# One load instead of two for the first weight block, a reordered row of small bias loads, and a later parameter transpose in a fused SSM + MLP kernel

## The chip, the cores and the metric

One core of a Trainium2 chip. The metric is the device time of one execution in microseconds (us), smaller is better. The sets of rounds ran on different chips (three are on record, and the median of the kernel before differs between them, 213.67 to 214.03 us), so times are compared within one set, and across sets only by their ratios.

"Traced" means one execution recorded by the hardware profiler. Times in a trace count from the start of its span. In all traced executions here the device time is the span plus 1.3 to 1.4 us.

## The reference

```python
# x: [1, 2048, 640] bf16; g is a gate for each row; a a complex diagonal SSM; b an MLP
g = sigmoid((x * gate_w).sum(-1, keepdims=True))
a = 2 * Re(h_seq @ C^T) + x * Dskip,  h_t = Lam_bar * h_{t-1} + B_bar @ x_t
b = gelu(x @ w1 + b1) @ w2 + b2       # w1: [640, 1728], w2: [1728, 640]
out = g * a + (1 - g) * b
```

`Lam_bar` and `B_bar` are worked out on chip from three vectors of 640 values (`Lambda_re`, `Lambda_im`, `log_dt`). These and `b1` are loaded as rows of one tile, `rows`, and turned into columns by one TensorE transpose, called the parameter transpose below.

## The kernel before

A small list scheduler orders the instructions on each engine by `prio` and by its own estimates, and puts waits where tiles depend on each other. (A semaphore is a counter: each DMA engine that moves a part of a load adds 1 to it when its part is done, in these traces 16 for a W1 block, 13 for b1's rows and 2 for the bias row, and the load has landed when the last one has.) What matters is the start: which loads are issued on which queue and in which order, and where in TensorE's order the parameter transpose stands.

```python
load("xna", "sp", ..., xn[0][:, :, 0:256], x2[0:512, 0:256]..., prio 0)
for h in range(2):                      # W1 block 0 (128 rows x 1024) in two loads, 1 KB pieces
    fs = slice(h * FW // 2, (h + 1) * FW // 2)
    load(f"w1_0{h}", "sp", ..., W1sb[:, 0, fs], B_w1[0:128, fs], [("w1", 0, h)], 0.1 + h, ...)
w1load(1, "sp", 1.3)                    # blocks 1 to 4: one load each, 2 KB pieces
w1load(2, "sp", 2)
xtrans(0, range(KN, KD), 3, 1.8)        # DMA transpose of x into xT, k = 2..4
w1load(3, "sp", 4)
w1load(4, "sp", 5)
# ... cut ...
# ACT queue: Lambda_re, Lambda_im, log_dt (5 rows each), b1 (13 rows), bias row b1b (1 row, 2 pieces)
load(nm, "act", "l_" + nm, rows[r0:...], src, [nm], prio=-100 + i, dur=0.4)
load("b1b", "act", "l_b1b", rows[RT:RT + 1, :]..., ["b1b"], prio=-96, dur=0.4)
# ... cut ...
op("cols", "pe", 0.3, list(ROWS) + ["b1b", "ident"], [("bank", 7)], f_cols, prio=9.5)  # parameter transpose
# ... cut: the first product x @ w1, 40 matmuls, k outermost, jf (8 PSUM banks) inside
op(f"m1_0_{jf}_{k}", "pe", d_mm(512), XK0[k] + [("w1", k) if k else ("w1", 0, jf // (NW // 2))], ...)
```

The first two k blocks of xT come from TensorE transposes of `xn`; k = 2 to 4 come from the DMA transpose. The parameter transpose uses PSUM bank 7, so it must stand ahead of the 15th matmul of the first product (called m1 here), which is the first to write that bank. At `prio` 9.5 it stands after 9 m1 matmuls. (One matmul is out of the k order: the one of bank 7 at k = 0 is put off to just before that of k = 1. So the first 7 matmuls need block 0, the 8th to 14th block 1, and the 17th is the first that needs block 2 and the DMA transpose of x.)

## Time and profile before

213.85 us median (213.85 to 213.9, 3 runs). The traced execution took 214.2 us, span 212.9 us.

| engine | busy us | share of the span |
|---|---|---|
| TensorE (PE) | 208.4 | 98% |
| VectorE (DVE) | 188.9 | 89% |
| ScalarE (ACT) | 111.3 | 52% |

From the profile page of the kernel before: the busy line and the first line of the chain that ended last.

```profile
PE 208.4 (98%) x1254; PEld 119.8 (56%) x1264; DVE 188.9 (89%) x262; ACT 111.3 (52%) x201; POOL 2.5 (1%) x10
PE 95%; DMA 2%; issue 1%; ACTq 1%; POOL 0%; DVE 0%; POOLq 0%
```

The list of waits of the kernel before, for TensorE (engine and line, what it waited for: us in total, times, longest):

```profile
PE ps L401 <- PEq L962: 0.8, 1, 0.8
PE ps L621 <- DMA W1sb<-in_B_w_dram: 0.4, 2, 0.2
PE ps L432 <- DMA rows<-in_B_b_dram: 0.3, 1, 0.3
PE ps L684 <- issue: 0.2, 1, 0.2
PE ps L621 <- DVE xT L419: 0.2, 1, 0.2
```

TensorE is the limit, and nearly all of its waits fall in the first 8 us. The timeline of the kernel before, TensorE from 3 us (start us, us, engine, line, operation, tiles, count, idle before and its releaser):

```profile
3.74 0.65 PE L413 MATMUL ps<-ident,xn 128*128 128x128 bf16 x8
4.64 1.04 PE L621 MATMUL ps<-xT,W1sb 128*128 128x512 bf16 x4 [0.25 <-DVE xT L419]
5.85 0.82 PE L621 MATMUL ps<-xT,W1sb 128*128 128x512 bf16 x3 [0.17 <-DMA W1sb<-in_B_w_dram]
6.92 0.61 PE L621 MATMUL ps<-xT,W1sb 128*128 128x512 bf16 x2 [0.25 <-DMA W1sb<-in_B_w_dram]
7.82 0.22 PE L432 MATMUL ps<-ident,rows 128*128 128x128 bf16 x1 [0.29 <-DMA rows<-in_B_b_dram]
7.87 6.85 PE L621 MATMUL ps<-xT,W1sb 128*128 128x512 bf16 x30
```

Four m1 matmuls, a gap, three, a gap, two, a gap, the parameter transpose, and from there on an unbroken stretch (L621 is m1, L432 the transpose). The timeline of the two issuing queues of the kernel before, for the first loads; consecutive loads of one tile are merged (x4 are W1's two halves, block 1 and block 2):

```profile
1.25 1.97 SPq L326 DMA_DIRECT2D W1sb<-in_B_w_dram  x4
3.27 1.54 SPq L333 DMA_TRANSPOSE xT<-in_A_x_dram  x1
0.97 0.57 ACTq L326 DMA_DIRECT2D rows<-in_A_Lambda_re_dram  x1
2.22 1.06 ACTq L326 DMA_DIRECT2D rows<-in_B_b_dram  x2
```

The last two of the ACT queue are b1's 13 rows (issued at 2.22) and the bias row (2.60).

### The profile page before, as it was taken

What the parts mean: (1) busy time and instruction counts of PE and PEld (TensorE: products, weight loads), DVE (VectorE), ACT (ScalarE), POOL (GpSimd) and SP (SyncE); (2) the same over time, 40 slices, a digit from 0 to 9 for tenths busy, and PEclk for the clock granted to TensorE, in tenths of its full rate; (3) what the DMA queues carried; (4) which work ended last, traced back from release to release, by engine and by line L of the source; (5) the groups of instructions that cost most, each with busy time, mean ns of one, the idle gap of its engine ahead of it and who ended that gap; (6) DMA issues with size and microseconds to landing.
All of it is one profiled execution on the core that took longest, in us unless ns stands there. A gap on an engine that the chain in (4) does not pass through costs nothing.

```text
span 212.9 us, 3113 instructions
## 1 busy us (share of the span) xinstructions
PE 208.4 (98%) x1254; PEld 119.8 (56%) x1264; DVE 188.9 (89%) x262; ACT 111.3 (52%) x201; POOL 2.5 (1%) x10
## 2 busy tenths in 40 slices
PE   8899999999999999999999999999999999999996
PEld 3344444444467776444466777544446777767773
DVE  2399999999999999999999959999999998999343
ACT  2389556678915324556963233555793444723330
POOL 1000000000000010000000001000000000000000
DMA  5999999998100004100000004000000000000011
GB/s 134 298 284 200 170 208 318 265 222 183 22 0 3 31 31 126 62 0 0 0 3 0 0 34 155 31 31 3 0 0 2 3 31 31 31 3 31 31 34 62
DMA packets 31434, 16.35 MB, mean 77 GB/s; under 512 B 22972, under 2 KB 30652, under 8 KB 31420
## 3 DMA queue, kind: packets, MB, share of 16 engines
q1 hardware_dynamic: 31072, 14.83, 29.2%
q0 software_dynamic: 288, 1.31, 1.9%
q8 instruction: 10, 0.16, 0.3%
q14 instruction: 4, 0.03, 0.0%
q10 hardware_dynamic: 60, 0.01, 0.0%
HBM read 7.63 MB, written 2.62 MB: 48 GB/s over the span
## 4 chain that ended last, share of the span: by engine, by line
PE 95%; DMA 2%; issue 1%; ACTq 1%; POOL 0%; DVE 0%; POOLq 0%
PE ps L771 27%; PE ps L641 22%; PE ps L819 20%; PE ps L684 20%; PE ps L621 3%; DMA rows<-in_B_b_dram 2%; PE ps L785 1%; PE ps L662 1%; ACTq L326 1%; DVE osb L852 0%; POOL io_i L382 0%; PE ps L432 0%; POOL rows L372 0%; POOL st_i L384 0%; POOL st_i L383 0%
## 5 line engine op out<-in xcount | busy, mean ns | idle before, releaser
L771 PE MATMUL ps<-W2sb,Gl 128*128 128x320 bf16 x416 | 59.2, 299 | 0.0
L771 PEld LDWEIGHTS ps<-W2sb,Gl 128*128 128x128 bf16 x416 | 40.3, 98 | 17.1 <-issue 1.1
L641 PE MATMUL ps<-xT,W1sb 128*128 128x512 bf16 x215 | 47.5, 379 | 0.3
L819 PE MATMUL ps<-CT,H 128*128 128x320 bf16 (+2 forms) x320 | 45.4, 299 | 0.0
L724 DVE TENSOR_TENSOR_SCAN W<-atab,V 128x1280 bf16<-128x1280 f32 x16 | 44.3, 2811 | 0.3
L684 PE MATMUL ps<-xT,BT 128*128 128x512 bf16 x196 | 43.1, 379 | 0.3 <-issue 0.2
L819 PEld LDWEIGHTS ps<-CT,H 128*128 128x128 bf16 x320 | 31.3, 98 | 12.2
L799 ACT ACTIVATE E<-ps,g1col 128x320 bf16<-128x320 f32 x32 | 16.3, 526 | 39.7 <-PE ps L771 26.0
L641 PEld LDWEIGHTS ps<-xT,W1sb 128*128 128x128 bf16 x220 | 21.5, 98 | 26.0
L648 ACT ACTIVATE Gl<-ps,cols 128x512 bf16<-128x512 f32 x44 | 29.6, 688 | 10.0 <-PE ps L641 10.0
L684 PEld LDWEIGHTS ps<-xT,BT 128*128 128x128 bf16 x200 | 19.5, 98 | 23.5 <-ACT Gt L670 0.4
L693 ACT ACTIVATE U<-ps 128x512 bf16<-128x512 f32 x40 | 23.8, 597 | 15.0 <-PE ps L684 14.9
L830 ACT ACTIVATE E<-ps,gcol 128x320 bf16<-128x320 f32 x30 | 15.8, 527 | 22.6 <-PE ps L819 22.6
L482 DVE TENSOR_TENSOR osb<-xg,E 128x640 bf16<-128x640 bf16 x15 | 7.3, 487 | 9.2 <-ACT E L830 8.2
L758 ACT ACTIVATE ps<-b2b 128x320 f32<-128x320 bf16 x32 | 14.1, 442 | 1.1
L838 DVE SCALAR_TENSOR_TENSOR xg<-xn,gcol,dsk 128x640 bf16<-128x640 bf16 x16 | 13.9, 883 | 0.4
L598 DVE SCALAR_TENSOR_TENSOR scr<-xn,gwb 128x640 bf16<-128x640 bf16 x16 | 13.2, 823 | 0.4
L482 DVE TENSOR_TENSOR V<-V,W 128x1280 bf16<-128x1280 bf16 x16 | 12.5, 822 | 0.3
L482 DVE TENSOR_TENSOR H<-H,V 128x1280 bf16<-128x1280 bf16 x16 | 12.5, 822 | 0.3
L482 DVE TENSOR_TENSOR V<-mr,U 128x2560 bf16<-128x2560 bf16 x8 | 11.9, 1489 | 0.2
L482 DVE TENSOR_TENSOR H<-c,W 128x2560 bf16<-128x2560 bf16 x8 | 11.9, 1489 | 0.1
L482 DVE TENSOR_TENSOR V<-s,W 128x2560 bf16<-128x2560 bf16 x8 | 11.9, 1485 | 0.0
(79 smaller groups left out, 98.5 us busy)
## 6 DMA issues: line engine op xcount, KB each, us to landing
out_dram<-osb SPq DMA_DIRECT2D x15, 160.0 KB, 1.8
W2sb<-in_B_w_dram SPq DMA_DIRECT2D x1, 2080.0 KB, 9.4
xn<-in_A_x_dram POOLq DMA_DIRECT2D x2, 640.0 KB, 4.7
W1sb<-in_B_w_dram SPq DMA_DIRECT2D x4, 256.0 KB, 4.8
xn<-in_A_x_dram SPq DMA_DIRECT2D x1, 640.0 KB, 8.0
W1sb<-in_B_w_dram SPq DMA_DIRECT2D x1, 480.0 KB, 5.7
W1sb<-in_B_w_dram SPq DMA_DIRECT2D x1, 400.0 KB, 5.8
xn<-in_A_x_dram SPq DMA_DIRECT2D x1, 384.0 KB, 6.2
```

What stands on the lines that cost most here:

```text
L482: return inc("dve", nc.vector.tensor_tensor(out=o, in0=a, in1=b, op=o_))
L641: t = nc.tensor.matmul(PS[bank][:, :], W1sb[:, k, jf * 128:(jf + 1) * 128], xT[q][:, k, :], start=(k == 0), stop=(k == KD - 1))
L648: return inc("act", nc.scalar.activation(Gl[q % 2][:, jf, :], PS[bank][:, :], ACT.Gelu_apprx_tanh, bias=b1col[:, jf:jf + 1]))
L684: t = nc.tensor.matmul(PS[bank][:, :], BT[:, ci, kd, k * 128:(k + 1) * 128], xT[q][:, kd, :], start=(kd == 0), stop=(kd == KD - 1))
L693: return inc("act", nc.scalar.activation(dst, src, ACT.Copy, scale=1.0 if ci == 0 else -1.0))
L724: t = inc("dve", nc.vector.tensor_tensor_scan(out=g[:, ci, :], data0=a, data1=v[:, ci, :], initial=0.0, op0=ALU.mult, op1=ALU.add))
L758: return inc("act", nc.scalar.activation(PS[bank][:, 0:HALF], b2b[:, cols], ACT.Copy))
L771: t = nc.tensor.matmul(PS[bank][:, 0:HALF], Gl[q % 2][:, jf, t4 * 128:(t4 + 1) * 128], W2sb[:, jf, cols], start=False, stop=False, skip_gr ...
L799: return inc("act", nc.scalar.activation(E1[c % NE][:, cols], PS[bank][:, 0:HALF], ACT.Copy, scale=g1col[:, c:c + 1]))
L819: t = nc.tensor.matmul(PS[bank][:, 0:n], H[b % NHB][:, ci, k, s * 128:(s + 1) * 128], CT[:, ci, k, cols], start=(i == 0), stop=(i == 2 * K ...
L830: return inc("act", nc.scalar.activation(E2[c % NE][:, cols], PS[bank][:, 0:HALF], ACT.Copy, scale=gcol[:, c:c + 1]))
L838: return inc("dve", nc.vector.scalar_tensor_tensor(out=xg[c % 2][:, :], in0=xn[q % 2][:, c % 4, :], scalar=gcol[:, c:c + 1], in1=dsk[:, :] ...
```

## The change

The intent: read W1's first block in longer pieces and with one issue fewer, get the single-row bias load out of the way early, and give the parameters two matmuls more time before TensorE has to wait for them.

```diff
-        for h in range(2):
-            fs = slice(h * FW // 2, (h + 1) * FW // 2)
-            load(f"w1_0{h}", "sp", f"l_w10{h}", W1sb[:, 0, fs], B_w1[0:128, fs], [("w1", 0, h)], 0.1 + h, dur=0.45, lat=2.0)
+        w1load(0, "sp", 1)
 ...
-             B_b1[nmain:F]...broadcast_to([1, 2, FL]), ["b1b"], prio=-96, dur=0.4)
+             B_b1[nmain:F]...broadcast_to([1, 2, FL]), ["b1b"], prio=-101, dur=0.4)
 ...
-        op("cols", "pe", 0.3, list(ROWS) + ["b1b", "ident"], [("bank", 7)], f_cols, prio=9.5)
+        op("cols", "pe", 0.3, list(ROWS) + ["b1b", "ident"], [("bank", 7)], f_cols, prio=11.5)
 ...   # m1 waits for the whole of block 0
-                op(f"m1_0_{jf}_{k}", ..., XK0[k] + [("w1", k) if k else ("w1", 0, jf // (NW // 2))], ...)
+                op(f"m1_0_{jf}_{k}", ..., XK0[k] + [("w1", k)], ...)
```

At the start, the order of instructions differs in just these points: one W1 load fewer on SP, the bias row first instead of last on ACT, and the parameter transpose after 11 instead of 9 m1 matmuls.

More of the change, by code (lines that the diff above doesn't have):

```diff
@@ L378, in bass_gated_mix__ssm_conv_s5__dense_activation_gelu__prompt_kernel @@
         load("b1b", "act", "l_b1b", rows[RT:RT + 1, :].rearrange("o (a p) -> o a p", a=2),
-             B_b1[nmain:F].rearrange("(o p) -> o p", o=1).unsqueeze(1).broadcast_to([1, 2, FL]), ["b1b"], prio=-96, dur=0.4)
+             B_b1[nmain:F].rearrange("(o p) -> o p", o=1).unsqueeze(1).broadcast_to([1, 2, FL]), ["b1b"], prio=-101, dur=0.4)
         def f_iota():
@@ L622, in f_mm @@
                                                       start=(k == 0), stop=(k == KD - 1)))
-                op(f"m1_0_{jf}_{k}", "pe", d_mm(512), XK0[k] + [("w1", k) if k else ("w1", 0, jf // (NW // 2))], [("bank", jf)] ,
+                op(f"m1_0_{jf}_{k}", "pe", d_mm(512), XK0[k] + [("w1", k)], [("bank", jf)] ,
                    f_mm, prio=pe_prio())
@@ L643, in f_mm @@
                     return inc("pe", t)
-                op(f"m1_{q}_{jf}", "pe", KD * d_mm(512), XT[q] + ([("w1", 0, 0), ("w1", 0, 1)] + [("w1", k) for k in range(1, KD)] if jf < NW else [("w1", "r", int(jf * 128 >= FM))]), [("bank", bank)], f_mm, prio=pe_prio())
+                op(f"m1_{q}_{jf}", "pe", KD * d_mm(512), XT[q] + ([("w1", k) for k in range(KD)] if jf < NW else [("w1", "r", int(jf * 128 >= FM))]), [("bank", bank)], f_mm, prio=pe_prio())
                 def f_ge(jf=jf, bank=bank):
```

## The prediction

> **What bounds the kernel.** TensorE. The page's busy table gives PE 208.4 of 212.9 us (98%), and the chain that ended last is 95% PE. The list of waits shows only five PE waits, all in the first 8 us: 0.8 us before the warm-up, then 0.25 (VectorE's copy of xT), 0.2 + 0.2 (W1 loads) and 0.3 (the load into `rows`). From the parameter transpose at 7.82 us on, PE runs practically without a gap up to the tail at 210.8 us. So only the start can pay, and at most about 1 us of it (idle from 4.39 to 7.87 us: 0.25 + 0.17 + 0.25 + 0.29), under 0.5% of the time.
>
> **The start, before** (timeline and landing records): xn part lands at 3.70; W1 block 0, first half 4.03, second half 5.81; block 1 6.87; block 2 7.56; xT's DMA transpose 9.05. PE: 4 matmuls at 4.64, 3 at 5.85, 2 at 6.92, parameter transpose at 7.82 (the single-row bias landed at 7.68, 4.4 us after its issue ended), then dense at 0.22 us each; the 12th m1 matmul starts near 8.31.
>
> The packet records show the bias row's two packets already running at 6.07 and 6.41 us, but its semaphore reaching its count only at 7.63/7.68, while the DMA transpose's first packets on all engines stand still from about 6.4 to 7.35. The Trainium skill, "DMA: Bandwidth & Descriptors", section on queues, rings and completion order, says that the completing increment lands only after every earlier write of that engine, across its queues; the trace agrees.
>
> **What the change does.** It removes one SP issue (0.42 us, spacing 0.54), so W1 blocks 1 and 2 and the DMA transpose are issued about 0.5 us earlier. 256 pieces of 1 KB (46 ns each) become 128 of 2 KB (84 ns): 0.74 to 0.67 us per engine, little. But the first m1 matmul now needs the whole block instead of its first half: I expect it to land at 4.6 to 5.6 us instead of 4.03, so PE starts m1 later (near 5.1), then runs 7 matmuls without the 5.68 gap. The bias row becomes early (near 3 us); b1's 13 rows become last, issued near 2.6 us, and land behind block 2 and the DMA transpose's stall, near 7.2 us. The transpose then stands after 11 matmuls.
>
> Estimate: 7 matmuls from 5.1 end at 6.7; block 1 near 6.5; four more end near 7.6; transpose 0.1 us more; 12th m1 matmul near 7.85 instead of 8.31. Gain near 0.4 us. The following matmuls need xT's DMA transpose (17th matmul, near 9.0 against landing 8.6 to 9.05), which caps it. Afterwards PE is the limit, so the gain should arrive at the end unchanged; VectorE's parameter chain starts at the same time or slightly earlier than 8.07 and has slack (1.0 us of ACT idle before the first gelu).
>
> **Prediction: 213.5 us, 80% range 213.0 to 214.1.** Faster by over 2%: 0.003; within 2%: 0.99; slower by over 2%: 0.007.
>
> **Right or wrong:** the first m1 matmul starts after 4.64 (W1 as releaser); no gap between matmuls 4 and 5; the transpose's release is W1 or the b1 load near 7.2 to 7.6; dense PE from there; the first gelu about 0.4 us earlier than 13.25; everything later shifted by that constant.
>
> **What would make it wrong:** the one-load block lands near the old second half's 5.81, cancelling the gain; b1's rows, spread on 13 engines, catch a straggler and land after 8 us, making it slower; the xT transpose becomes a new wait at the 17th matmul; or the stall is shorter and the gain nearer 0.8 us.

## The result, and the profile after

213.93 us median (213.69 to 214.44, 4 runs), against 213.85 us (213.47 to 213.9, 4 runs) before: ratio 1.0011, 95% interval 0.9989 to 1.0032. Here and below a ratio is made from the runs of both kernels in the same rounds; it is not quite the ratio of the medians quoted.

The time lies in the predicted range, but the gain of 0.4 us, the point of the argument, is not there. The trace alone would have said otherwise: its span is 212.6 us against 212.9. But the traced execution of the kernel before took 214.2 us, 0.35 us more than its median; that of the changed kernel, 213.91 us, is a usual one. The page of the changed kernel (busy line and chain):

```profile
PE 208.7 (98%) x1254; PEld 120.3 (57%) x1264; DVE 189.2 (89%) x262; ACT 111.3 (52%) x201; POOL 2.5 (1%) x10
PE 95%; DMA 2%; ACTq 1%; issue 1%; POOL 0%; DVE 0%; POOLq 0%
```

The list of waits of the changed kernel, TensorE, and its timeline from 3 us:

```profile
PE ps L399 <- PEq L960: 0.8, 1, 0.8
PE ps L430 <- DMA rows<-in_B_b_dram: 0.3, 1, 0.3
PE ps L682 <- issue: 0.2, 1, 0.2
```

```profile
3.69 1.03 PE L411 MATMUL ps<-ident,xn 128*128 128x128 bf16 x8
4.68 2.94 PE L619 MATMUL ps<-xT,W1sb 128*128 128x512 bf16 x11
7.97 0.22 PE L430 MATMUL ps<-ident,rows 128*128 128x128 bf16 x1 [0.35 <-DMA rows<-in_B_b_dram]
8.03 6.42 PE L619 MATMUL ps<-xT,W1sb 128*128 128x512 bf16 x28
```

The two W1 waits are gone from the list, and the wait for a row load is still there. And the eight small transposes at L411 take 1.03 us where before they took 0.65: TensorE ran at half speed there. The queues of the changed kernel:

```profile
1.26 1.62 SPq L326 DMA_DIRECT2D W1sb<-in_B_w_dram  x3
2.92 2.01 SPq L333 DMA_TRANSPOSE xT<-in_A_x_dram  x1
0.97 1.19 ACTq L326 DMA_DIRECT2D rows<-in_B_b_dram  x1
3.22 0.33 ACTq L326 DMA_DIRECT2D rows<-in_B_b_dram  x1
```

The bias row's issue takes 1.19 us at the head of the queue (Lambda_re in that place took 0.57), so b1's 13 rows, now last, are issued at 3.22 us, 0.62 us later than the last load before, and behind the DMA transpose instead of ahead of it. When the loads land, by the semaphore records of the two traces (time of the last DMA engine's increment):

| us | before | changed |
|---|---|---|
| W1 block 0 | 4.03 and 5.81 (halves) | 4.30 |
| W1 block 1 | 6.87 | 6.54 |
| W1 block 2 | 7.56 | 7.28 |
| last row load | 7.68 (bias row) | 7.73 (b1's 13 rows) |
| xT, DMA transpose | 9.05 | 8.79 |
| 12th m1 matmul starts | 8.30 | 8.03 |
| first B projection matmul starts | 19.95 | 19.68 |

The B projection is what TensorE does after the first product. From its first matmul to the end of the span it took 192.91 to 192.93 us in every one of the 14 traces. So the whole effect of any of these kernels is one number: when the B projection starts. The device time is that number plus 194.2 to 194.3 us.

### The profile page after: what moved, and what is told of

It reads as the page before. It is cut to its first block, busy times and chain, and to the rows that moved or that the text cites. A ratio compares the mean times of both kernels' runs of the same rounds, so it can differ in the third digit from the quotient of the medians.

```text
span 212.6 us, 3112 instructions
## 1 busy us (share of the span) xinstructions
PE 208.7 (98%) x1254; PEld 120.3 (57%) x1264; DVE 189.2 (89%) x262; ACT 111.3 (52%) x201; POOL 2.5 (1%) x10
## 4 chain that ended last, share of the span: by engine, by line
PE 95%; DMA 2%; ACTq 1%; issue 1%; POOL 0%; DVE 0%; POOLq 0%
PE ps L769 27%; PE ps L639 22%; PE ps L817 20%; PE ps L682 20%; PE ps L619 3%; DMA rows<-in_B_b_dram 2%; PE ps L783 1%; PE ps L660 1%; ACTq L326 1%; DVE osb L850 0%; POOL io_i L380 0%; PE ps L430 0%; POOL rows L370 0%; POOL st_i L382 0%; POOL st_i L381 0%
```

## The experiments

Three theories were on the table. **A**: the gain is real and comes from two matmuls moved ahead of a wait whose end hardly moves; the wait is for whatever row load stands last in the ACT queue. **B**: the difference of the two traces is scatter. **C** (later): the reordering and the one-load block work against each other. "Before" stands for the kernel before, on the same chip in the same rounds.

### The two kernels again

No edit. `before_again` expected:

> The kernel before, unchanged, to see how far two executions of one kernel differ. Theory A (the change shifts TensorE's dense stretch by a fixed 0.27 us, because two matmuls move ahead of a wait of nearly unchanged end): the second m1 group again starts at 14.56 us within 0.1, the last bias load again lands near 7.7 us. Theory B (the 0.27 us between the two traces is the scatter of one execution against another, from late DMA packets and from when the TensorE clock is granted): the start scatters by 0.3 us or more. Time ratio to itself 1.000 within 0.002 in both.

Measured: 213.86 us median (213.46 to 214.11, 6 runs), ratio to itself 1.0000 (0.9986 to 1.0013). In its trace the B projection starts at 19.79 us (0.16 earlier than in the other trace of the same kernel) and the bias row lands at 7.19 us, not 7.7.

`after_again` expected:

> The changed kernel, unchanged. Theory A: the second m1 group starts at 14.29 us within 0.1, ratio 0.9987 (0.27 of 213.85 us). Theory B: the start lies anywhere between 14.1 and 14.8, ratio 1.000 within 0.001. In both the parameter transpose waits for b1's 13 rows (landing near 7.7 us), since they have taken the place at the end of the ACT queue that the bias row had.

Measured: 214.05 us median (213.12 to 214.6, 6 runs), ratio 1.0009 (0.9988 to 1.0029). B projection at 19.42 us, rows at 7.42 us, parameter transpose waiting 0.3 us for them. The second m1 group started at 13.81 us, outside what theory A allowed. A single trace does not carry a 0.3 us argument here: block 2 landed at 7.05 and 7.56 us in two executions of one kernel. Theory A in its strict form fell.

### Parts alone

`only_cols`, the kernel before with

```diff
-        op("cols", ..., f_cols, prio=9.5)
+        op("cols", ..., f_cols, prio=11.5)
```

> The kernel before with only the parameter transpose two matmuls later. Theory A says that this part alone carries the gain: bias row landing stays near 7.7 us, 11 matmuls are done before it (if block 1 lands by 6.9: the 11th ends near 7.9), so the transpose hardly waits, the 12th m1 matmul starts near 8.0 instead of 8.30, the second group near 14.25 to 14.3; ratio 0.9985 to 0.999. If instead the one-load block or the queue order carries it, the second group starts near 14.56 as before.

Measured: 213.78 us (213.15 to 213.94, 6 runs), ratio 0.9992 (0.9978 to 1.0007). The bias row landed at 7.70 us, the transpose ran at 7.83 us without a wait in the list, B projection at 19.70 us. The trace is as theory A has it; the time is not clear of noise.

`only_order`, the kernel before with the bias row at `prio=-101`:

> The kernel before with only the bias row moved to the front of the ACT queue. If the order costs: the first issue takes 1.19 us, b1's 13 rows are issued at 3.2 us, land at 7.4 to 7.9 us, the transpose at its old place waits longer than before, B projection start 20.0 to 20.3 us (before: 19.79 and 19.96), ratio 1.001 to 1.002. If the order is what the change gains by, the transpose waits less and the ratio is under 0.999.

Measured: 213.89 us (213.7 to 214.15, 5 runs) against 214.03, ratio 0.9992 (0.998 to 1.0005). The first issue did take 1.19 us and b1's rows were issued at 3.22 us and landed at 7.44 us, but the expected loss is not there: B projection at 19.82 us (the transpose did wait longer, 0.51 us against 0.29). With block 0 in two loads the DMA transpose is issued at 3.45 us, after the rows, and the rows landed 0.12 us after block 2, as closely as the bias row did before.

`only_load`, the kernel before with the one-load block (and m1 waiting for all of it):

> The kernel before with only the one-load block. SP's later issues come about 0.5 us earlier. Theory A: block 0 lands near 4.3 us (the changed kernel: 4.27 and 4.30), before TensorE needs it, so the wait for the second half (5.3 to 5.8 us) goes, but the gain is absorbed by the wait for the bias row (landing 7.1 to 7.5): parameter transpose near 7.4 to 7.6 instead of 7.65 to 7.82, B projection start near 19.6 to 19.8, ratio 0.999 to 1.000.

Measured: 213.9 us (213.59 to 214.15, 5 runs), ratio 0.9992 (0.9979 to 1.0005). Block 0 at 4.37 us, bias row at 7.43 us, transpose waiting 0.4 us for it, B projection at 19.71 us: the W1 gaps go and are swallowed by the wait for the row, as expected.

### What holds the row loads: the DMA transpose moved back

`late_transpose`, the changed kernel with

```diff
-        xtrans(0, range(KN, KD), 3, 1.8)
-        w1load(3, "sp", 4)
-        w1load(4, "sp", 5)
+        w1load(3, "sp", 2.5)
+        w1load(4, "sp", 2.7)
+        xtrans(0, range(KN, KD), 3, 1.8)
```

> The changed kernel with W1 blocks 3 and 4 issued ahead of xT's DMA transpose. Theory A2 (block 2's and the parameter rows' completions are held up because the DMA transpose's first packets stand still on all engines until the last engine has finished its W1 packets): block 2 lands by about 6.3 us except for a late engine and b1's rows near 6.3 us instead of 7.73, and the transpose of the parameters no longer waits; the still stand moves to some 8.5 us. Rival A3 (the rows are late because of their place in the queues alone): they land at 7.5 to 7.7 as before. Either way xT's DMA transpose lands after 10 us and stops TensorE at the 17th m1 matmul by 0.8 to 1.3 us, so this kernel is slower by about 0.5 to 1 us; it is for diagnosis.

Measured: 214.89 us (214.6 to 215.27, 4 runs), ratio 1.0051 (1.0035 to 1.0066). The two of its TensorE waits that matter:

```profile
PE ps L619 <- DMA xT<-in_A_x_dram: 1.2, 1, 1.2
PE ps L430 <- DMA rows<-in_B_b_dram: 0.6, 1, 0.6
```

The loss is as expected; the rows are not where theory A2 had them (6.3 us): they landed at 7.62 us, where the rival A3 had them. They were issued (3.23 us) after block 3 (2.93 us); that they came late because they stood behind it is likely, but was not tested. Block 2, however, now arrives spread out: 12 of its 16 DMA engines had finished by 6.41 us and the last at 7.27 us, while in the changed kernel 14 of 16 report between 7.08 and 7.28 us. So the DMA transpose does hold up the completions of block 2; that it is also what holds the rows in the changed kernel, this run does not show.

The packet records of all 14 traces show the same pattern. The first 256-byte packets of the DMA transpose begin while a slow DMA engine still works on W1; they then stand still for up to 1.46 us, and those that stand all end within 22 to 52 ns of each other, 0.17 to 0.25 us after the last W1 packet. Nine of the traces (the second column gives the median end of the standing packets):

| us | last W1 packet ended | standing packets ended | block 2 landed | last row load landed |
|---|---|---|---|---|
| before | 7.17 | 7.37 | 7.56 | 7.68 |
| before_again | 6.66 | 6.86 | 7.05 | 7.19 |
| changed | 6.89 | 7.10 | 7.28 | 7.73 |
| after_again | 6.64 | 6.85 | 7.14 | 7.42 |
| after_third | 6.54 | 6.76 | 6.96 | 7.33 |
| cols_and_load | 6.58 | 6.77 | 6.97 | 7.05 |
| cols_and_load_again | 6.27 | 6.48 | 6.69 | 6.86 |
| cols_and_order | 6.39 | 6.62 | 6.91 | 7.06 |
| late_transpose | 8.49 | 8.69 | 7.27 | 7.62 |

(In the last line the standing packets come after block 4, so block 2 and the rows escape them.) In the trace of before the bias row's two packets ran at 6.07 and 6.41 us, but the semaphore was complete only at 7.68. The Trainium skill, "DMA: Bandwidth & Descriptors", section "Queues, rings and completion order", says that the increment lands only after every earlier write from that DMA engine, across its queues; the table agrees. What makes one engine slow on the W1 blocks (single packets of 0.4 to 1.4 us where 84 ns is usual) no run here settles.

The table shows a second thing: with the reordering and the one-load block together (changed, after_again, after_third) the rows land 0.28 to 0.45 us after block 2; in every other kernel of the table but late_transpose it is 0.08 to 0.17 us (0.12 to 0.19 in the traces of `only_cols`, `only_order` and `only_load`).

### The rows off the ACT queue

`bias_pool`, the changed kernel with both b1 loads issued by GpSimd:

```diff
-            load(nm, "act", ..., prio=-100 + i, dur=0.4)
-        load("b1b", "act", ..., ["b1b"], prio=-101, dur=0.4)
+            load(nm, "pool" if nm == "b1a" else "act", ..., prio=-50 if nm == "b1a" else -100 + i, dur=0.4)
+        load("b1b", "pool", ..., ["b1b"], prio=-51, dur=0.4)
```

> The changed kernel with both b1 loads issued by GpSimd (after its iotas, at 1.4 to 3.2 us; its two xn loads each took 0.75 to 0.88 us to issue) and the three Lambda and dt rows alone on the ACT queue. Theory A (in both kernels the parameter transpose waits for whatever row load stands last in the ACT queue, since that one is issued at 2.6 to 3.2 us, behind W1 block 2, and its completion is held until the DMA transpose gets going near 7 us): all rows land before 5.5 us, the parameter transpose follows the 11th m1 matmul without a wait, the first B projection matmul starts at 19.1 to 19.4 us instead of 19.4 to 19.7, ratio 0.997 to 0.999. Rival B (the scatter of the W1 packets sets everything, the rows only follow it): the 12th m1 matmul then waits for W1 block 2 or xT instead and the start stays at 19.4 to 19.8, ratio 1.000 within 0.001.

Measured: 213.44 us (213.09 to 213.72, 6 runs) against 214.03, ratio **0.9972 (0.9959 to 0.9985)**, by its ratio the best and better than both kernels (the changed kernel was not in these rounds). Its timeline:

```profile
4.75 1.69 PE L619 MATMUL ps<-xT,W1sb 128*128 128x512 bf16 x7 [0.16 <-DVE xT L417]
6.67 1.04 PE L619 MATMUL ps<-xT,W1sb 128*128 128x512 bf16 x4 [0.24 <-DMA W1sb<-in_B_w_dram]
7.54 0.22 PE L430 MATMUL ps<-ident,rows 128*128 128x128 bf16 x1
7.60 6.63 PE L619 MATMUL ps<-xT,W1sb 128*128 128x512 bf16 x28
```

The rows land by 6.21 us (expected 5.5, a miss in size; the B projection starts at 19.46 us, just outside the expected 19.1 to 19.4), and the transpose follows the 11th matmul without a wait. The rival B (the rows only follow) fails: the row wait was a real limit in this form of the kernel. The next limits show at once: W1 block 1 (0.24 us of wait at 6.67), and at the 17th matmul the DMA transpose of xT (landed 8.83, matmul at 8.88).

`pool_only`, the kernel before with only that edit:

> The kernel before with only both b1 loads moved to GpSimd's queue; block 0 in two loads, parameter transpose at its old place. If the wait for the last row load is the whole limit: rows land by 6.3 us, no wait at the transpose, ratio 0.997 to 0.998 as with one-load block and later transpose beside it (0.9972). If the one-load block matters once the rows wait no longer (SP issues 0.5 us earlier, so xT lands earlier): 0.998 to 0.9995, with TensorE waiting for the second half of block 0 and at the 17th m1 matmul for xT near 9.0 us.

Measured: 213.69 us (213.01 to 214.02, 6 runs) against 213.67, ratio 0.9996 (0.9981 to 1.001). The rows landed at 4.94 us and were waited for by nobody, and still nothing was gained in the mean. In its trace TensorE ran at half speed until 6.5 us, and the 17th matmul came just after xT had landed (9.19 and 9.15 us). Taking the row wait away paid together with the one-load block, which brings SP's later issues 0.5 us forward, and the later transpose (`bias_pool`), and not alone; which of the two it needs was not run, and the two ratios are from different chips.

### Undoing the reordering

`cols_and_load`, the changed kernel with the bias row last again (`prio=-96`):

> The changed kernel with the bias row last in the ACT queue again, so one-load block and later transpose without the reordering. Theory A with the addition that the reordering costs (the row load that now comes last has 13 pieces on 13 DMA engines instead of 2 on 2, and the first issue takes 1.19 us instead of 0.57): the last row load is issued at 2.6 us instead of 3.22 and lands within 0.15 us of block 2 (7.0 to 7.5) instead of 0.3 to 0.45 us after it; the B projection starts 0.1 to 0.3 us earlier than in the changed kernel, near 19.4, ratio to before 0.9985 to 0.9995. If the reordering is neutral: same as the changed kernel within 0.0005.

Measured: 213.78 us (213.39 to 214.08, 6 runs) against 214.03, ratio 0.9985 (0.9971 to 0.9999). The bias row landed at 7.05 us, 0.08 us after block 2. In this trace TensorE ran at half speed until 6.8 us, so the B projection came at 19.84 us, late for what the loads allowed. Repeated beside the changed kernel, as `cols_and_load_again`:

> The changed kernel with the bias row last again, repeated beside the changed kernel. Theory C: ratio near 0.9985, 0.001 to 0.002 below the changed kernel on the same chip; last row load within 0.2 us of block 2. If the order is neutral: both within 0.0007 of each other.

Measured: 213.3 us (213.08 to 213.72, 6 runs) against 213.67, ratio 0.9986 (0.9974 to 0.9997). B projection at 18.80 us, the earliest of all. So two of the three parts give a gain, twice, with intervals that just exclude 1.

`cols_and_order`, the kernel before with reordering and later transpose, block 0 in two loads:

> The kernel before with the reordering and the later transpose, block 0 still in two loads. Theory C: with the extra SP issue the DMA transpose is issued at 3.45 us, after b1's rows at 3.22 us, so the rows land within 0.15 us of block 2 and the ratio is 0.998 to 0.9993, better than the changed kernel. If the reordering itself costs (its first issue takes 1.19 us, and 13 rows wait for 13 engines): ratio 1.000 to 1.001 as the changed kernel.

Measured: 213.44 us (213.24 to 213.74, 5 runs), ratio 0.999 (0.9978 to 1.0001), rows 0.15 us after block 2, as theory C expected. Both pairs of parts that were tried are at or below 0.999; the three together are not. (One-load block and reordering without the later transpose was not run.)

### The changed kernel a third time

> The changed kernel again, on the same chip as the next three, because its 10 runs so far average 213.97 us, although its two traces start the B projection 0.1 to 0.5 us earlier than the two of the kernel before. Theory C (reordering and one-load block work against each other: the DMA transpose is now issued at 2.92 us, ahead of b1's 13 rows at 3.22 us, so these rows are held not only until block 2 is done but 0.3 us and in some executions more beyond it): ratio again 1.000 to 1.001, rows 0.25 to 0.6 us after block 2. If those earlier runs were only scatter: ratio near 0.9987.

Measured, on the same chip: 213.83 us median, but 213.57 to **215.89** (6 runs), ratio 1.0032 (0.9999 to 1.0065). In these same rounds `cols_and_load_again` averaged 213.35 us and the changed kernel 214.39; without its two slow executions (215.46 and 215.89) the other four still average 213.75. So in these rounds the reordering cost 0.4 us, and the slow executions more on top. This time the traced execution was a slow one, 215.46 us. Its TensorE waits and timeline:

```profile
PE ps L619 <- DMA W1sb<-in_B_w_dram: 0.9, 1, 0.9
PE ps L399 <- PEq L960: 0.8, 1, 0.8
PE ps L682 <- issue: 0.2, 1, 0.2
```

```profile
3.58 1.03 PE L411 MATMUL ps<-ident,xn 128*128 128x128 bf16 x8
5.49 4.18 PE L619 MATMUL ps<-xT,W1sb 128*128 128x512 bf16 x11 [0.88 <-DMA W1sb<-in_B_w_dram]
9.51 0.22 PE L430 MATMUL ps<-ident,rows 128*128 128x128 bf16 x1
9.57 6.42 PE L619 MATMUL ps<-xT,W1sb 128*128 128x512 bf16 x28
```

And the same stretch of `cols_and_load_again`, one of the fastest executions:

```profile
4.66 2.60 PE L619 MATMUL ps<-xT,W1sb 128*128 128x512 bf16 x11
7.09 0.22 PE L430 MATMUL ps<-ident,rows 128*128 128x128 bf16 x1
```

Eleven matmuls took 4.18 us instead of 2.60. In the slow execution block 0 landed at 5.36 us (15 of its 16 engines by 4.22; one engine was late), TensorE sat idle for 0.88 us, and then the first nine m1 matmuls started 0.38 to 0.43 us apart, until 9.1 us; only then came 0.216 us. Rows and DMA transpose landed early here (7.33 and 8.44 us) and were waited for by nobody.

This is the TensorE clock. The Trainium skill, "TensorE: Matmul & The Clock Gate", Part 1, says that the array runs at half rate until it has been busy for a window of about 3.4 us, that the window runs freely, so that the moment of the switch varies from run to run, and that 512-column matmuls start 426.7 ns apart at half rate and 215.7 ns at full. These traces agree on the spacings. They also show how the switch varies: in the other 13 it had come by a time between 3.9 and 6.8 us; the one execution with a 0.88 us hole reached it at about 9.1 us, 3.6 us after the hole. That the hole spoiled one window is an inference from that page and this one trace, in keeping with both. Most of the loss is the half-rate stretch: eight spacings at 0.21 us extra each are 1.7 us, an estimate from the two spacings. Against `cols_and_load_again`, whose B projection starts 2.42 us earlier (18.80 against 21.22), 0.83 us are the later first matmul and 1.58 us the slower eleven.

## Why the prediction was right or wrong

The range (213.0 to 214.1) held the time, 213.93 us, and "within 2%" was as good as certain, because TensorE is busy 98% and only the first 8 us were touched. That it held says nothing for the argument: it is 1.1 us wide, nearly three times the argued gain, and no gain at all (213.85 us) lies in it too. That only the start counts is shown: 192.91 to 192.93 us from the B projection to the end in every trace. But the argued gain of 0.4 us did not come. Over 16 timed executions the changed kernel has a median of 213.93 us and a mean of 214.13; the kernel before, over the 32 of the same rounds, has 213.81 and 213.78 (over all 43, 213.84 and 213.86).

Step by step, as the prediction put it:

- **"It removes one SP issue, so W1 blocks 1 and 2 and the DMA transpose are issued about 0.5 us earlier."** In part. Block 1 was issued 0.46 us earlier (1.80 against 2.26), but block 2 only 0.34 us (2.45 against 2.79) and the DMA transpose 0.35 us (2.92 against 3.27), since block 1's issue took 0.60 us beside the long bias-row issue; without the reordering (`only_load`) the shift was 0.47 to 0.53.
- **"I expect [block 0] to land at 4.6 to 5.6 us, so PE starts m1 later (near 5.1)."** Wrong for the usual execution: 4.30 and 4.27 us, before TensorE needed it at 4.68. Right only in the slow one (5.36).
- **"b1's 13 rows become last, issued near 2.6 us, and land near 7.2 us."** The issue was at 3.22 us, because the load at the head of the queue took 1.19 us to issue, and the landing at 7.73, 7.42 and 7.33 us. This is the mis-sized term of the sum in the first trace: the transpose there waited 0.35 us, at 7.97 instead of the predicted 7.7 or so, and the 12th matmul came at 8.03 instead of 7.85, 0.18 us less gain.
- **"12th m1 matmul near 7.85 instead of 8.31."** 8.03, 7.76 and 9.57 us in three executions, against 8.30 and 8.14.
- **"Gain near 0.4 us" and "213.5 us".** The gain was read from one trace and taken off the median, but that trace was of an execution of 214.2 us, 0.35 us slower than the median of 213.85. From the 12th matmul to the B projection it took 11.65 us in both kernels' traces, and the device time is 194.2 to 194.3 us more. So a 12th matmul at 7.85 us is an execution of about 213.75 us (an estimate from these sums), only 0.1 us under the median before; about 0.3 us of the forecast gain were the scatter of the one traced execution. With the 12th matmul at 8.03 the same sum gives 213.93, the measured median.
- **"The following matmuls need xT's DMA transpose, which caps it."** Not in these traces: the 17th matmul ran at 9.10 us, 0.3 us after the landing. It did become the next wait in `bias_pool` (about 0.2 us) and in `only_cols` (0.14 us).
- **"Afterwards PE is the limit, so the gain should arrive at the end unchanged."** Right.
- **What was missing altogether:** the state of TensorE's clock at the start, and the spread. The two halves of block 0 were not just slower: in the six traces with two halves, the first half is there at 3.96 to 4.20 us, before TensorE needs it at about 4.7. With the whole block as the condition, one late DMA engine out of 16 left TensorE idle for 0.88 us before its clock had been released, and that execution took 215.46 us, 1.6 us over the median of its rounds. (A late block 0 did stand on the prediction's list of what would make it wrong; the spread and the clock did not.) Of 16 executions of the changed kernel 4 took over 214.4 us (up to 215.89); of 43 of the kernel before none did (up to 214.38). The line at 214.4 was drawn after the fact, and two of the four (214.44 and 214.6) lie barely above it.

What stays open: only one of those four slow executions was traced, so that the others have the same cause is not shown. Nor is it settled why the slow ones are found in the changed kernel and not in the four timings of `only_load`, `cols_and_load` (twice) and `bias_pool`, which have the one-load block too (23 executions, none more than 0.1 us above their rounds' mean of before). In all four traces of kernels with both the bias row first and the one-load block, 2 to 6 of block 0's packets that start between 2.8 and 3.2 us stand for 0.2 to 0.8 us, about when the bias row's two packets run (2.76 to 3.05 us); in the four traces with that block but the bias row not first there is one such packet, of 0.21 us. That makes the bias row at the head of the queue a suspect, no more: in three of those four traces block 0 landed at 4.27 to 4.35 us all the same, no later than without the reordering (4.28 to 4.41), in the two traces with the bias row first and block 0 in two loads no packet stands that long there, and no run took it apart.

So the change is a sum of two parts that are useful together (one load, later transpose: 0.9985 and 0.9986; each alone 0.9992, not clear of noise) and a third that takes it back (with the reordering: 1.0011, 1.0009, 1.0032). It would not have shown as a loss by itself: `only_order` is at 0.9992. That the reordering takes the gain back rests on the times; how it does so (rows held 0.28 to 0.45 us after block 2, slow executions) is in part argued.

## What to carry to other kernels

Where a tile is filled by several small loads, the last of them is the one that is waited for, and moving another one out of its way only changes which one is last; here it paid to move them to an idle queue (GpSimd, 0.3% with the other two parts) and not to reorder them within the queue. Before one large load is made the only condition of the first matmuls, ask what its latest execution costs: in one trace here a late block 0 cost its own 0.88 us and a long half-rate stretch besides. (It is no rule: four timings with the one-load block, the best of the study among them, showed no such execution.) When a gain is read from a trace, check first how the traced execution's time lies to the median from which the gain will be taken. And where executions scatter by 0.5 us, compare distributions and read several traces: the first trace of the changed kernel looked 0.3 us better while its mean was 0.2 us worse in the same rounds.

## What the Trainium skill lacked or had wrong

- "DMA: Bandwidth & Descriptors", section "DMA Transpose (X-bar)": it does not say that a DMA transpose's first packets stand still until the ordinary packets issued ahead of it are done on the slowest DMA engine. Here they ended 0.17 to 0.25 us after the last W1 packet in 14 of 14 traces, after standing for up to 1.46 us, and completions of other loads on those engines were held with them (bias row: packets at 6.07 and 6.41 us, landing 7.68 us).
- The same page, section "Queues, rings and completion order", has each engine take turns between the queue rows, a whole packet at a time, but gives no time for how long a small load waits for its turns. Here the bias row, the fifth load on the ACT queue, issued at 2.60 us, ran at 6.07 and 6.41 us, when 210 and 237 of the 256 pieces of W1 blocks 1 and 2 (issued on SP at 2.26 and 2.79 us) were done. Whether that is turn-taking or something else, no run here settles.
- The same page gives no issue times for loads on few engines. Here a load of one row in two pieces took 1.19 us to issue at the head of the ACT queue and 0.68 us at its end, against 0.27 to 0.57 us for loads of 5 rows and 0.31 to 0.36 us for one of 13.
- "TensorE: Matmul & The Clock Gate" covers the half-rate start well (0.43 and 0.216 us here), but its figure of 500 ns either way for the moment of the switch is too narrow: with the first warm-up matmul at 0.78 us in every trace, 13 traces reached full rate at times between 3.9 and 6.8 us (its count of 6, 11 or 14 slow matmuls in runs of one kernel is the better guide). It does not warn that a hole in the ramp may cost another window: in the one trace with 0.88 us of idle, full rate came at about 9.1 us. The mean granted clock in the profiles read 1.00 in all of them, so the start-to-start spacing is what to look at.
